# Weight splits on other engines, hidden copies on ScalarE, and a fourth raw tile in a fused attention and two-layer feed-forward kernel

## Chip, cores and metric

The kernel runs on one core of a Trainium2 chip. The metric is the device time of one execution in microseconds (us), lower is better. Five engines work side by side, each on its own queue in order: TensorE (PE, matmuls; PEld is its weight load), VectorE (DVE), ScalarE (ACT), GpSimd (POOL) and SyncE (SP), which here issues all DMAs.

## The reference, cut to what matters

```python
# q, k, v: (4, 8, 576, 64), f: (4, 8, 576), all float32; x: 2304 tokens x 512
scores = q @ k.T / 8 + (cum_i - cum_j)      # cum = cumsum(log(clip(f, 1e-4, 1)))
scores = where(causal, -1e9, scores)
attn = exp(scores - max) / (sum + 1e-9)
x = attn @ v                                # heads side by side: 2304 x 512
h = x @ w_in;  g = h * tanh(log1p(exp(h)));  x = g @ w_out      # layer 1, d_ff 2048
h = x @ w2_in; g = h * cos(h);               out = g @ w2_out   # layer 2
```

The four weight matrices arrive as 64-bit floats. The kernel makes two float32 values of each weight, a high part and the remainder, and likewise of each activation, and multiplies in three matmuls (high x high, high x low, low x high).

## The kernel before, in words

**Stages.** Attention works on jobs (a pair of heads of one batch) and on blocks of 128 queries. Beside it run "hidden units": one unit is 12 matmuls that make one 128-wide slice of layer 1's hidden values for 256, 288 or 320 tokens (L161). There are 128 of them; those that attention leaves over (31 or 32) run after it, from about 380 us on, and take all eight PSUM banks in turn. Each pair of units is copied from PSUM into a tile `hs`, the first half by ScalarE (L186), the second by VectorE (L188), and stored to `hd` in HBM by SP (L189). Then `ffn_units` goes through layer 1 in steps: it loads `hl` from `hd` (L223, seven steps ahead), applies the activation (L298), splits the result into gh (L324, ScalarE) and gl (L329, VectorE), and multiplies (L256). Layer 2 follows with L161, L301 to L329 and L264.

**Splitting the weights.** `split_weights` cuts each of the four matrices into 16 pieces of 512 KB. A piece is loaded into a `raw` tile (L109, on SP) and then goes through VectorE (L128, L129), GpSimd (L133, for the first matrix, called early) or ScalarE (L137, the others), VectorE (L138), ScalarE (L142, the high part wih or woh) and GpSimd (L143, the low part wil or wol, by subtraction). Only after L143 is the raw tile free for the next load. There are two raw tiles during attention and three after it; loads are issued one piece ahead during attention and two after it (`PF`). The early matrix is split during attention; then w1o (layer 1, out), w2i and w2o.

**Who calls it when.** During attention one piece is asked for every second block. In the loop over the left hidden units (L871) w1o's pieces are asked for in two of three units; from the fourth-last unit on, steps of `ffn_units` are interleaved. Then the loop over `ffn_units` asks for w2i and w2o.

**Order on the queues.** The program is written in this order, but a planner at build time arranges each engine's instructions by modelled durations; on the chip every engine then keeps that order. `issue_after(x)` puts an edge in that plan: the block's instructions on x's engine come behind x. `marks["v1"]` is the last VectorE instruction of a hidden unit or step, so the conversions' VectorE instructions stand behind it; the early ones stand behind the last softmax reduction (`marks["ttr"]`).

**Memory.** `ident`, `maskt` and `mask2` are used by attention alone but lie in the pool `const`, which stays for the whole kernel. Attention's own pool `att` is closed at L840, before the later raw pool is opened (L843).

```python
        PF = 1 if early else 2
                key = "ttr" if early else "v1"
                nc.gpsimd.tensor_tensor(out=lo[sl], in0=f(high), in1=f(hi[sl]), op=ALU.subtract)
    rawp = ctx.enter_context(tc.tile_pool(name="raw", bufs=3))
        if n % 3 != 2:
            next(w1o, None)
```

Of the kernel before, what the change touches and what calls it, by code (L numbers as in the profile page):

```python
# [9 lines left out]
F32 = mybir.dt.float32  # L10
F32R = mybir.dt.float32r
I32 = mybir.dt.int32
AF = mybir.ActivationFunctionType
ALU = mybir.AluOpType
# [21 lines left out]
def f(ap):  # L36
    return ap.bitcast(F32)
# [3 lines left out]
def tile_attention_two_ffn(  # L41
# [12 lines left out]
    nc = tc.nc  # L54
    B, H, S, D = q.shape
# [14 lines left out]
    const = ctx.enter_context(tc.tile_pool(name="const", bufs=1))  # L70
# [2 lines left out]
    raw_sb = ExitStack()  # L73
    rawp = raw_sb.enter_context(tc.tile_pool(name="raw0", bufs=2))

    ident = const.tile([128, 128], F32, name="ident")
    maskt = const.tile([128, S], F32, name="maskt")
    mask2 = const.tile([128, 320], F32, name="mask2")
    quarter = const.tile([128, 1], F32, name="quarter")

    hd = dram.tile([128, NJ, NT], F32, name="hd")
# [8 lines left out]
    marks, cums = {}, []  # L90

    def split_weights(layer, nm, pool, early=False):
        wi, wo = (w1_in, w1_out) if layer == 1 else (w2_in, w2_out)
        nb, nn = (NK, 256) if nm == "i" else (2, DM)
        per = 512 // nn
        pieces = []
        for c in range(NCH):
            if nm == "i":
                src = wi.bitcast(I32)[:, 512 * c : 512 * c + 512].rearrange("(b p) n -> p b n", p=128)
            else:  # L100
                src = wo.bitcast(I32)[256 * c : 256 * c + 256, :].rearrange("(b p) n -> p b n", p=128)
            pieces += [(c, src, u) for u in range(0, nb, per)]
        raws = {}

        def load(i):
            if i < len(pieces):
                c, src, u = pieces[i]
                raws[i] = rawp.tile([128, per, nn, 2], I32, tag="raw", name="raw")
                nc.sync.dma_start(out=raws[i].rearrange("p b n t -> p b (n t)"), in_=src[:, u : u + per])  # L109

        PF = 1 if early else 2
        with tc.issue_after(marks["cum"].ins):
            for i in range(PF):
                load(i)
        for i, (c, src, u) in enumerate(pieces):
            load(i + PF)
            raw = raws.pop(i)
            if u == 0:
                W[layer, c, nm] = tuple(
                    pool.tile([128, nb, nn], F32R, tag=f"w{nm}{x}{c}", name=f"w{nm}{x}{c}") for x in "hl"  # L120
                )
            hi, lo = W[layer, c, nm]
            with ExitStack() as hold:
                key = "ttr" if early else "v1"
                if key in marks:
                    hold.enter_context(tc.issue_after(marks[key].ins))
                high, low = raw[:, :, :, 1], raw[:, :, :, 0]
                nc.vector.tensor_scalar(out=low, in0=low, scalar1=29, scalar2=None, op0=ALU.logical_shift_right)  # L128
                nc.vector.scalar_tensor_tensor(  # L129
                    out=low, in0=high, scalar=-0x80000000, in1=low, op0=ALU.bitwise_and, op1=ALU.bitwise_or  # L130
                )
                if early:
                    nc.gpsimd.tensor_scalar(  # L133
                        out=f(high), in0=f(high), scalar1=REBIAS, scalar2=1.0, op0=ALU.mult, op1=ALU.mult
                    )
                else:
                    nc.scalar.activation(out=f(high), in_=f(high), func=AF.Copy, scale=REBIAS)  # L137
                nc.vector.scalar_tensor_tensor(  # L138
                    out=high, in0=high, scalar=3, in1=low, op0=ALU.logical_shift_left, op1=ALU.bitwise_or
                )  # L140
                sl = (slice(None), slice(u, u + per))
                nc.scalar.activation(out=hi[sl], in_=f(high), func=AF.Copy)  # L142
                nc.gpsimd.tensor_tensor(out=lo[sl], in0=f(high), in1=f(hi[sl]), op=ALU.subtract)  # L143
            if u + per == nb:
                converted[layer, c, nm] = clock["m"]
            yield

    def ripe(*key):
        return key in converted and clock["m"] - converted[key] >= WEIGHT_LAG
# [6 lines left out]
    def in_products(o, layer, j, xh, xl):  # L156
        wh, wl = weight(layer, j, "i")
        for kk in range(NK):
            wsl = (slice(None), kk, slice(128 * (j % 2), 128 * (j % 2) + 128))
            for i, (a, b) in enumerate(((wh, xh), (wh, xl), (wl, xh))):  # L160
                nc.tensor.matmul(  # L161
                    o, lhsT=a[wsl], rhs=b[:, kk, :],
                    start=(kk == 0 and i == 0), stop=(kk == NK - 1 and i == 2),
                )

    def hidden_units(tiles, p, hbank, ready):
        todo = {tl: 0 for tl in tiles}
        while todo:
            can = [tl for tl in todo if ready(sum(tl))]
            have = [tl for tl in can if ripe(1, todo[tl] // 2, "i")]  # L170
            if not can or not (have or attention_over):
                yield None
                continue
            t0, T = have[0] if have else min(can, key=todo.get)
            b, at = divmod(t0, S)
            xh, xl = (xb[b][:, x, :, at : at + T] for x in range(2))
            j0 = todo[t0, T]
            todo[t0, T] += 2
            if todo[t0, T] == NJ:
                del todo[t0, T]  # L180
            hs = p.tile([128, 2, 320], F32, tag="hs", name="hs")[:, :, 0:T]
            for j in (j0, j0 + 1):
                t = hbank()[:, 0:T]
                in_products(t, 1, j, xh, xl)
                if j == j0:
                    nc.scalar.activation(out=hs[:, 0], in_=t, func=AF.Copy)  # L186
                else:
                    marks["v1"] = nc.vector.tensor_copy(hs[:, 1], t)  # L188
                    nc.sync.dma_start(out=hd[:, j0 : j0 + 2, t0 : t0 + T], in_=hs)  # L189
                yield j  # L190

    def ffn_units(first, second, p, hlp, xp, hbank, abank, open_second):
# [552 lines left out]
            yield ("step", m, nxt[0] - m if nxt else 1)  # L745

    nc.scalar.preload_act_table_set("natural_log_exp_and_others")
    make_identity(nc, ident)
    nc.gpsimd.memset(quarter, 0.25)

    def make_masks():
        nc.gpsimd.memset(maskt, 0.0)
        nc.gpsimd.affine_select(
            out=maskt[:, S - 128 : S], in_=maskt[:, S - 128 : S], pattern=[[-1, 128]], base=0,
            channel_multiplier=1, compare_op=ALU.is_ge, fill=MASKED,
        )
        nc.gpsimd.memset(mask2, 0.0)
        for x in (0, 64):
            nc.gpsimd.affine_select(
                out=mask2[x : x + 64, 256:320], in_=mask2[x : x + 64, 256:320], pattern=[[-1, 64]], base=0,  # L760
                channel_multiplier=1, compare_op=ALU.is_ge, fill=MASKED,
            )
# [19 lines left out]
    def hbank():  # L782
        banks["n"] += 1
        n = banks["n"]
        if banks["wide"] and n % 2 == 0:
            return abank(n // 2 % NK)
        n = n // 2 if banks["wide"] else n
        if attention_over and n % 2:
            return psx.tile([128, 512], F32, tag="hx", name="hx", bufs=2)
        return psf.tile([128, 512], F32, tag="h", name="h", bufs=2)  # L790
# [8 lines left out]
        xps[i] = xsb[i].enter_context(tc.tile_pool(name=f"x{i}", bufs=1, side="right"))  # L799
    att_sb, att_ps, late_sb = ExitStack(), ExitStack(), ExitStack()  # L800
    ap = att_sb.enter_context(tc.tile_pool(name="att", bufs=2, side="right"))
    psf = ctx.enter_context(tc.tile_pool(name="ffps", bufs=1, space=PSUM))
    psa = att_ps.enter_context(tc.tile_pool(name="attps", bufs=6, space=PSUM))

# [3 lines left out]
    decay_tables(ap)  # L808
    att = attention_units(ap, bank)
    weights = split_weights(1, "i", w0p, early=True)  # L810
    done, done_tokens, attention_over = [], 0, False
    hid = hidden_units(hidden, hsp, hbank, lambda n: done_tokens >= n)
    credit = 0.0
    issued = 0
# [25 lines left out]
    att_sb.close()  # L840
    xsb[0].close()
    raw_sb.close()
    rawp = ctx.enter_context(tc.tile_pool(name="raw", bufs=3))  # L843
    attention_over = True
    psx = ctx.enter_context(tc.tile_pool(name="ffxps", bufs=1, space=PSUM))
    w1p = ctx.enter_context(tc.tile_pool(name="w1", bufs=1))
# [22 lines left out]
    banks["wide"] = True  # L869
    left = sum(NJ for _ in hidden) - issued  # L870
    for n, _ in enumerate(hid):  # L871
        if n % 3 != 2:
            next(w1o, None)
        if n == left - NK - 1:
            banks["wide"] = False
        if n >= left - 4:
            for kind, _ in ffn:
                if kind == "out":
                    break
# [38 lines left out]
```

## Time and profile before

| what | us |
|---|---|
| median of 3 runs | 1036.1 (1035.66 to 1036.38) |
| the profiled execution | 1035.64 |
| its span, first to last instruction | 1033.9 |
| TensorE busy | 1002.0 |
| VectorE busy | 595.3 |
| ScalarE busy | 526.4 |
| GpSimd busy | 232.6 |

The profile is of one execution. Busy time counts instructions that compute; issuing DMAs, branches and semaphores are not in it. "Granted clock" is the share of TensorE's full speed that the chip allowed. A number in brackets behind an instruction is the time that its engine sat idle before it, with what ended the wait. The chain of waits is followed back from the last instruction, at each step to what released it.

### The profile page before, as it was taken

How to read it: one execution, taken by the hardware profiler on the slowest of the kernel's cores; microseconds unless marked ns; L12 is line 12 of the kernel's file. 1: busy time of each engine (PE TensorE's matmuls, PEld its weight loads, DVE VectorE, ACT ScalarE, POOL GpSimd, SP SyncE). 2: the span in 40 equal slices, each digit the busy share in tenths (PEclk: the TensorE clock that was granted, in tenths of full speed). 3: DMA queues.
4: the chain of work that ended last, by engine and by line, in shares of the span. 5: the costliest groups of instructions: out<-in, count | busy, mean ns of one | idle time of the engine just before them, and what ended most of it. 6: DMA issues, size and time to landing. Idle time of an engine off the chain costs nothing.

```text
span 1033.9 us, 16608 instructions
## 1 busy us (share of the span) xinstructions
PE 1002.0 (97%) x5852; PEld 858.2 (83%) x5852; DVE 595.3 (58%) x1350; ACT 526.4 (51%) x1126; POOL 232.6 (22%) x303
## 2 busy tenths in 40 slices
PE   5997999999999999989999999999999999999998
PEld 4676789899999999878898888888888888888887
DVE  5875985555555437747773387665544444454454
ACT  4774765565555445456664466444333333333343
POOL 7655653323233104412220032111000000000000
PEclk9998999999999999999999999999999999999999
DMA  4663442323322158757885456202100200110010
GB/s 121 173 180 94 133 129 75 88 78 99 92 68 70 58 194 265 230 157 244 293 279 162 132 192 220 85 21 82 41 1 21 102 1 0 41 42 1 1 42 21
DMA packets 118494, 111.77 MB, mean 108 GB/s; under 512 B 66700, under 2 KB 87180, under 8 KB 118412
## 3 DMA queue, kind: packets, MB, share of 16 engines
q1 hardware_dynamic: 118412, 110.72, 35.0%
q8 instruction: 46, 0.75, 0.3%
q14 instruction: 36, 0.29, 0.1%
HBM read 77.49 MB, written 33.18 MB: 107 GB/s over the span
## 4 chain that ended last, share of the span: by engine, by line
PE 88%; POOL 4%; issue 3%; DVE 2%; DMA 2%; ACT 1%; SPq 0%; POOLq 0%; ACTq 0%; DVEq 0%
PE h L161 25%; PE acc L264 19%; PE acc L256 10%; PE hx L161 10%; PE s L637 5%; PE hx L256 4%; PE h L256 4%; PE s L527 4%; PE s L613 3%; PE s L470 2%; POOL wol L143 2%; PE s L521 2%; PE s L601 1%; DMA stk<-cumd 1%; DMA raw<-in_moe_w_out_dram 0%
## 5 line engine op out<-in xcount | busy, mean ns | idle before, releaser
L161 PE MATMUL h<-xb,wih 128*128 128x288 f32 (+2 forms) x848 | 183.0, 305 | 2.0 <-ACT wih L142 1.5
L161 PEld LDWEIGHTS h<-xb,wih 128*128 128x128 f32 x848 | 138.2, 190 | 8.2 <-issue 2.5
L161 PE MATMUL h<-xb,wil 128*128 128x288 f32 (+2 forms) x424 | 126.4, 301 | 4.9 <-POOL wil L143 4.9
L575 POOL TENSOR_SCALAR s<-s,sm 128x128 f32<-128x128 f32 (+4 forms) x144 | 83.7, 593 | 134.9 <-DVE sm L573 105.1
L264 PE MATMUL acc<-woh,gh 128*128 128x512 f32 x288 | 112.9, 392 | 0.0
L264 PE MATMUL acc<-woh,gl 128*128 128x512 f32 x288 | 112.3, 391 | 0.0
L264 PE MATMUL acc<-wol,gh 128*128 128x512 f32 x288 | 112.0, 389 | 0.0
L562 ACT ACTIVATE s<-s,mx 128x128 f32<-128x128 f32 (+4 forms) x144 | 83.6, 581 | 52.2 <-DVE mx L558 46.3
L558 DVE CUSTOM_DVE_ANT_0 s<-s,maskt 128x128 f32<-128x128 f32 (+4 forms) x144 | 66.9, 483 | 57.1 <-PE s L527 28.0
L329 DVE TENSOR_TENSOR gl<-hl,gh 128x512 fp32r<-128x512 f32 x72 | 58.5, 813 | 62.9 <-ACT gh L324 57.7
L161 PE MATMUL hx<-x,wih 128*128 128x512 f32 (+1 forms) x320 | 92.7, 369 | 0.0
L143 POOL TENSOR_TENSOR wol<-raw,woh 128x512 fp32r<-128x512 f32 x32 | 45.9, 1437 | 200.6 <-ACT woh L142 118.1
L315 ACT ACTIVATE n<-n 128x512 f32<-128x512 f32 (+1 forms) x80 | 47.1, 589 | 86.2 <-DVE n L309 86.1
L161 PE MATMUL h<-x,wih 128*128 128x512 f32 (+1 forms) x320 | 91.0, 369 | 0.0
L161 PEld LDWEIGHTS h<-xb,wil 128*128 128x128 f32 x424 | 80.4, 190 | 6.2 <-POOL wil L143 5.1
L329 DVE TENSOR_TENSOR gl<-e,gh 128x512 fp32r<-128x512 f32 (+1 forms) x80 | 54.0, 676 | 52.0 <-ACT gh L324 51.9
L308 DVE TENSOR_SCALAR n<-e 128x512 f32<-128x512 f32 (+1 forms) x80 | 32.7, 409 | 85.4 <-ACT e L301 84.9
L324 ACT ACTIVATE gh<-e 128x512 fp32r<-128x512 f32 (+1 forms) x80 | 47.0, 588 | 53.8 <-DVE e L320 49.2
L256 PE MATMUL acc<-gl,woh 128*128 128x512 f32 (+1 forms) x192 | 68.5, 358 | 0.7 <-DVE gl L329 0.7
L256 PE MATMUL acc<-gh,wol 128*128 128x512 f32 (+1 forms) x192 | 68.5, 358 | 0.0
L161 PEld LDWEIGHTS hx<-x,wih 128*128 128x128 f32 x320 | 58.4, 188 | 11.0
L161 PEld LDWEIGHTS h<-x,wih 128*128 128x128 f32 x320 | 58.4, 188 | 10.9
(119 smaller groups left out, 2164.3 us busy)
## 6 DMA issues: line engine op xcount, KB each, us to landing
hl<-hd SPq DMA_DIRECT2D x72, 256.0 KB
raw<-in_moe_w_in_dram SPq DMA_DIRECT2D x32, 512.0 KB
raw<-in_moe_w_out_dram SPq DMA_DIRECT2D x32, 512.0 KB
hd<-hs SPq DMA_DIRECT2D x48, 288.0 KB
yd<-stage SPq DMA_DIRECT2D x32, 256.0 KB
x<-yd SPq DMA_DIRECT2D x32, 256.0 KB
natk<-in_k_dram SPq DMA_DIRECT2D x32, 144.0 KB
out_dram<-stage SPq DMA_DIRECT2D x18, 256.0 KB
```

Source lines behind the costliest of these rows:

```text
L143: nc.gpsimd.tensor_tensor(out=lo[sl], in0=f(high), in1=f(hi[sl]), op=ALU.subtract)
L161: nc.tensor.matmul(o, lhsT=a[wsl], rhs=b[:, kk, :], start=(kk == 0 and i == 0), stop=(kk == NK - 1 and i == 2),)
L256: nc.tensor.matmul(acc[ti][d][:, 0:T], lhsT=a[dsl], rhs=b[:, gs], start=(start and i == 0), stop=(end and i == 2),)
L264: nc.tensor.matmul(acc[ti][m], lhsT=a[:, ms], rhs=b[:, j % 2, :], start=(start and i == 0), stop=(end and i == 2),)
L315: nc.scalar.activation(out=t, in_=t, func=AF.Sin, scale=TWO_PI)
L324: gmark[n] = nc.scalar.activation(out=gh, in_=e, func=AF.Copy)
L329: marks["v1"] = nc.vector.tensor_tensor(out=gl, in0=st.pop(n)[0], in1=f(gst[n][0]), op=ALU.subtract)
L527: marks["score"] = nc.tensor.matmul(o, lhsT=tails[x][j] if both else st[x][:, j, QS[i] : w], rhs=st[x + 1][:, j, c0:c1], start=(x == 0 and ...
L558: marks["ttr"] = nc.vector.tensor_tensor_reduce(out=s[:, c0:c1], in0=o, in1=mk, scale=-1.0, scalar=prev, op0=ALU.add, op1=ALU.min, accum_o ...
L562: nc.scalar.activation(out=s[:, 0:w], in_=s[:, 0:w], func=AF.Exp, scale=-1.0, bias=mx, accum_out=sm[:, j : j + 1])
L575: nc.gpsimd.tensor_scalar(out=s[:, 0:w], in0=s[:, 0:w], scalar1=sm[:, j : j + 1], scalar2=1.0, op0=ALU.mult, op1=ALU.mult)
L637: pair = nc.tensor.matmul(t[64 * j : 64 * j + 64, c0:width], lhsT=vt[jb][keys, c, j], rhs=pt[keys, j, c, c0:width], start=(c == 0), stop=( ...
```

## The change

- The subtraction L143 of the early pieces and of w1o's pieces goes from GpSimd to VectorE; w2i and w2o keep it on GpSimd.
- In the hidden units after attention both halves of `hs` are copied by ScalarE, and ScalarE issues the store to `hd`. During attention nothing changes there. w1o's pieces are held behind the last such copy (`marks["hs"]`, on ScalarE) in place of `marks["v1"]`.
- `ident`, `maskt` and `mask2` lie in attention's pool. The raw pool after attention has four tiles in place of three, and loads run three pieces ahead in place of two.
- In the loop over the left hidden units a piece of w1o is asked for in every second unit, in place of two of three.

```diff
-    ident = const.tile([128, 128], F32, name="ident")
-    maskt = const.tile([128, S], F32, name="maskt")
-    mask2 = const.tile([128, 320], F32, name="mask2")
...
-        PF = 1 if early else 2
+        PF = 1 if early else 3
...
-                key = "ttr" if early else "v1"
+                beside = (layer, nm) == (1, "o")
+                key = "ttr" if early else "hs" if beside else "v1"
...
-                nc.gpsimd.tensor_tensor(out=lo[sl], in0=f(high), in1=f(hi[sl]), op=ALU.subtract)
+                sub = nc.vector if early or beside else nc.gpsimd
+                sub.tensor_tensor(out=lo[sl], in0=f(high), in1=f(hi[sl]), op=ALU.subtract)
...
-                if j == j0:
-                    nc.scalar.activation(out=hs[:, 0], in_=t, func=AF.Copy)
+                if j == j0 or attention_over:
+                    marks["hs"] = nc.scalar.activation(out=hs[:, j - j0], in_=t, func=AF.Copy)
                 else:
                     marks["v1"] = nc.vector.tensor_copy(hs[:, 1], t)
-                    nc.sync.dma_start(out=hd[:, j0 : j0 + 2, t0 : t0 + T], in_=hs)
+                if j > j0:
+                    store = nc.scalar if attention_over else nc.sync
+                    store.dma_start(out=hd[:, j0 : j0 + 2, t0 : t0 + T], in_=hs)
...
+    ident, maskt, mask2 = (
+        ap.tile([128, w], F32, name=n, bufs=1) for n, w in (("ident", 128), ("maskt", S), ("mask2", 320))
+    )
+    make_identity(nc, ident)
+    nc.gpsimd.memset(quarter, 0.25)
...
-    rawp = ctx.enter_context(tc.tile_pool(name="raw", bufs=3))
+    rawp = ctx.enter_context(tc.tile_pool(name="raw", bufs=4))
...
-        if n % 3 != 2:
+        if n % 2 == 0:
             next(w1o, None)
```

## Rows read from the trace of the kernel before

**Rows 1.** The page: busy us, share, instructions; granted clock in 40 slices, in tenths

```profile
PE 1002.0 (97%) x5852; PEld 858.2 (83%) x5852; DVE 595.3 (58%) x1350; ACT 526.4 (51%) x1126; POOL 232.6 (22%) x303
...
PEclk9998999999999999999999999999999999999999
```

**Rows 2.** Stretches: us; busy PE, PEld, DVE, ACT, POOL; clock; DMA share, GB/s

```profile
25.00:150.00 125.00, 114.61 (x840) 91.62 (x839) 95.91 (x291) 83.81 (x229) 78.32 (x103) 0.97 0.53 141
87.00:94.00 7.00, 0.89 (x5) 0.69 (x5) 2.24 (x8) 2.43 (x6) 6.65 (x9) 0.88 0.13 28
94.00:100.00 6.00, 6.00 (x30) 5.89 (x32) 0.78 (x4) 0.38 (x1) 1.48 (x3) 0.57 0.40 131
...
380.00:443.00 63.00, 58.10 (x407) 55.63 (x406) 44.01 (x69) 33.56 (x61) 23.84 (x16) 1.00 0.80 249
448.00:1024.00 576.00, 576.00 (x2710) 482.10 (x2709) 313.77 (x505) 268.81 (x458) 43.09 (x32) 1.00 0.28 93
```

**Rows 3.** Who waited for whom, TensorE: us in total, times, longest

```profile
PE h L161 <- POOL wil L143: 4.9, 1, 4.9
...
PE hx L161 <- ACT hs L186: 2.5, 1, 2.5
...
PE acc L256 <- ACT gh L324: 2.1, 1, 2.1
...
PE acc L256 <- DVE gl L329: 0.7, 1, 0.7
```

**Rows 4.** GpSimd in order of time: start us, us, line, instruction [idle before]

```profile
91.91 0.50 POOL L507 CAST stkr<-stkr 64x384 fp32r<-64x384 f32 x1
92.50 1.29 POOL L143 TENSOR_TENSOR wil<-raw,wih 128x512 fp32r<-128x512 f32 x1
```

**Rows 5.** VectorE in order of time, around 90 us

```profile
95.96 0.42 DVE L188 COPY hs<-h 128x256 f32<-128x256 f32 x1 [5.91 <-PE h L161]
```

**Rows 6.** VectorE in order of time, a subtract without GpSimd beside it

```profile
448.20 0.69 DVE L329 TENSOR_TENSOR gl<-hl,gh 128x512 fp32r<-128x512 f32 x1 [3.54 <-ACT gh L324]
```

**Rows 7.** Chain of waits, matmuls of the hidden units: start us, us, what

```profile
93.84 5.28 PE h L161 x20
...
374.51 3.18 PE h L161 x24
```

**Rows 8.** One line's instructions, L129: duration ns min/median/max

```profile
L129 DVE SCALAR_TENSOR_TENSOR raw<-raw x64: 675/694/1853, 21.7 to 705.5; 128x512 int32<-128x512 int32 x64
```

**Rows 9.** Chain of waits, 370 to 450 us

```profile
431.27 1.33 POOL wol L143
...
432.62 4.89 DMA raw<-in_moe_w_out_dram
...
441.34 0.53 ACT gh L324
```

**Rows 10.** GpSimd in order of time, the last subtract of w1o

```profile
441.42 1.30 POOL L143 TENSOR_TENSOR wol<-raw,woh 128x512 fp32r<-128x512 f32 x1 [3.25 <-ACT woh L142]
```

**Rows 11.** Groups of VectorE, 380 to 443 us: busy us, mean ns, idle before

```profile
L129 DVE SCALAR_TENSOR_TENSOR raw<-raw 128x512 int32<-128x512 int32 x16 | 14.1, 880 | 0.4
```

**Rows 12.** TensorE in order of time, first L256 and last before its wait

```profile
431.48 0.40 PE L256 MATMUL acc<-gh,woh 128*128 128x512 f32 x1
...
439.46 0.39 PE L256 MATMUL acc<-gh,wol 128*128 128x512 f32 x1
```

**Rows 13.** Stretches of 2 us behind the wait

```profile
444.00:446.00 2.00, 2.00 (x7) 1.52 (x6) 0.67 (x1) 0.46 (x1) 0.00 (x0) 0.50 0.93 303
446.00:448.00 2.00, 2.00 (x8) 1.58 (x6) 0.00 (x0) 0.46 (x1) 0.00 (x0) 0.66 0.89 330
```

**Rows 14.** Groups of ScalarE, 380 to 443 us: hs copies

```profile
L186 ACT ACTIVATE hs<-hx 128x288 f32<-128x288 f32 x9 | 3.6, 397 | 0.6 <-ACT hs L186 0.6
```

**Rows 15.** L189, DMA issues on SP: duration ns min/median/max

```profile
L189 SPq DMA_DIRECT2D hd<-hs x64: 359/381/869, 55.4 to 439.6; - x64
```

**Rows 16.** Who waited for whom, all engines

```profile
DVE raw L138 <- ACT raw L137: 14.5, 28, 0.8
```

More of the change, by code (lines that the diff above doesn't have):

```diff
@@ L747, in tile_attention_two_ffn @@
     nc.scalar.preload_act_table_set("natural_log_exp_and_others")
-    make_identity(nc, ident)
-    nc.gpsimd.memset(quarter, 0.25)
     def make_masks():
```

## The prediction

> **What bounds the kernel now.** I read the busy times first. TensorE is busy for 1002.0 of 1033.9 us, and the granted clock is full in most of the 40 slices [rows 1]. Nearly all of the time is matmul work that the change does not touch; only the 31.9 us in which TensorE is idle, and the time at the lower clock, can go. The table by stretches says where these are: 10.4 us of idle time between 25 and 150 us, of which 6.1 from 87 to 94; a granted clock of 0.57 from 94 to 100; 4.9 us idle from 380 to 443; nothing at all from 448 to 1024 [rows 2]. The rest is the start and the tail, which the change leaves alone. The list of TensorE's waits puts names to the holes: once 4.9 us for the wil subtract on GpSimd (L143), and later 2.5 us for an hs copy on ScalarE, 2.1 for gh and 0.7 for gl [rows 3].
>
> **Place A, 87 to 100 us (the early subtracts go to VectorE).** GpSimd's order shows why wil is late: the subtract starts at 92.50, right behind a copy that ends at 92.41, and takes 1.29 [rows 4]; that copy follows the memsets of attention's second stack. VectorE is idle for the 5.91 us before 95.96, so from 90.05 on, because it waits for TensorE [rows 5]. There a subtract of the same shape (gl, L329) takes 0.69 us when nothing holds it up [rows 6]. So wil comes at about 90.8 where it came at 93.8: 3.0 us earlier. The 20 matmuls behind it took 5.28 us, to 99.12 [rows 7], at a clock of 0.57 over their stretch [rows 2]; at full clock they need 5.28 x 0.57 = 3.0. If the shorter pause keeps the clock, they end at 93.8, a gain of 5.3. The scores behind them need GpSimd's copy of 92.41, so 99.12 - 92.41 = 6.7 is the most that can come of it; if the clock still falls, 3.0 remains. I take 5.3.
>
> Against this stands VectorE's added work. All 16 early subtracts lie between 25 and 150 us: 16 x 0.69 = 11.0 us, or 16 x 0.865 = 13.8 at the mean of L129, the two-input VectorE instruction of the same size that runs beside GpSimd all through the kernel [rows 8]. VectorE is busy for 95.91 of these 125 us [rows 2], and of the 29.1 free ones some 9 lie in the hole itself and go with it. What VectorE loses is on the path only where TensorE already waits for it, and outside the hole TensorE's waits in this stretch are 10.4 - 6.1 = 4.3 us. I charge two subtracts, 1.4; the ends are 0 (all in free time) and 13.8 (all on the path). GpSimd gets back 16 x 1.29 us, but its normalises (L575) stand in no long wait of TensorE, so I credit nothing. Place A: 5.3 - 1.4 = 3.9.
>
> **Place B, 380 to 448 us (hidden units beside w1o's split).** The chain of waits at the seam reads: a GpSimd subtract ends at 432.60, only that frees a raw tile, its load takes 4.89, VectorE and ScalarE convert, and not before 441.34 can ScalarE turn to gh, which stands behind them on its queue [rows 9]. The subtract of the piece starts at 441.42 and takes 1.30 [rows 10], so one turn of a raw tile is 442.72 - 432.60 = 10.1 us, and three tiles give a piece per 3.4 us. The walk over the hidden units (24 matmuls, two units, in 3.18 us [rows 7]) asks for two pieces per three units, one per 2.4 us: the split never keeps up.
>
> After the change a turn has the same load and conversions and a VectorE subtract of 0.69 in place of 1.30: 9.5 us, by four tiles 2.4 us a piece. Besides, GpSimd has nothing left in this stretch, so L129, 0.880 on average here against a median of 0.694, loses 16 x 0.19 = 3.0 us [rows 8, 11]. The code asks for one piece per two units, 3.2 us; 16 pieces take 51 us from about 380, and TensorE ends the hidden units at 431.5 and has acc work until 439.9 [rows 12]. So a piece is ready before it is asked for, with about 8 us to spare before gh is due. The raw loads also stop queueing behind the hd stores on SP's queue. Freed are the waits of 2.5, 2.1 and 0.7 [rows 3] and the low clock behind the last: two stretches of 2 us at 0.50 and 0.66 lose 1.0 + 0.7 [rows 13]. That is 7.0 us.
>
> The cover is ScalarE. It is busy for 33.56 of the 63 us [rows 2] and gets 16 more hs copies at 0.40 [rows 14] and 16 stores. No row shows ScalarE issuing a DMA; SP needs 0.359 to 0.869 us, median 0.381, for each of these [rows 15], and a store could cost nothing if ScalarE only hands it on, so 0 to 13.9 us for all. I take SP's median, 6.1, for it is the same instruction. 33.6 + 6.4 + 6.1 = 46 of about 57 us: full, but not the bound. Every hs copy now stands in order behind L137 and L142, which wait for VectorE; the eight PSUM banks that the hidden units take in turn (12.7 us of TensorE work) cover that. I leave 1.0 for one such wait. Place B: 6.0, with 7.0 as the upper end and, if ScalarE falls behind, a loss as the lower.
>
> **The rest at nothing.** Identity and masks take 4 x (128 + 576 + 320) = 4096 bytes per partition, just one raw tile, so what is allocated behind stays where it was; the first instructions on GpSimd are the same. Three pieces ahead in the splits of w2i and w2o, and hs copies that no longer stand between VectorE's conversions, fall where TensorE is never idle [rows 2]. If the loads crowd out hl's, those still run seven steps ahead.
>
> **A rule against the change.** L129 takes 0.675 us at least and 1.853 at most [rows 8]. The Trainium skill, "SBUF — State Buffer", section "SBUF: two separate sides", says that a VectorE instruction with two SBUF inputs and a GpSimd one that reads SBUF lock each other out for a whole instruction. The trace agrees as far as L129's spread goes. By that rule an early subtract can stand still behind a normalise, while place B, without GpSimd, is free of it; the third rival prices this from the rows.
>
> **Sum.** The profiled execution took 1035.64 us (span 1033.9 and 1.7 around it), 0.46 below the median of 1036.1. 1035.64 - 3.9 - 6.0 = 1025.7, on the scale of the median 1026.
>
> **The rivals.**
> *Only B comes.* The subtracts cost attention what the hole gave back. For it: VectorE is busy for 77% from 25 to 150 us. Against: only 4.3 us of TensorE's waits there lie outside the hole. 1036.1 - 6.0 = 1030.
> *Only A comes.* ScalarE becomes the bound from 380 to 443, hs copies and gh come late, and TensorE waits at the seam as before. For it: 46 of 57 us on a queue in order. Against: the margin of 8 us. 1036.1 - 3.9 = 1032.
> *Slower: VectorE becomes the bound of attention.* Each early subtract waits in VectorE's order for ScalarE's wih (0.5 us, as L138 waited for ScalarE 14.5 us in 28 cases [rows 16]) and takes the 1.85 of L129's longest: 16 x 2.35 = 37.6 us. If half of the 29.1 free us is bound up in the dependences, TensorE starves for 37.6 - 14.5 = 23.1, less 5.3 and 6.0: 1048. It decides from (14.5 + 11.3) / 16 = 1.6 us for each subtract; the rows say 0.69 to 0.87.
> *It does not do what it says.* The order on each engine is drawn up at build time from modelled durations, and the new one can put a wait of the same size elsewhere. Against: the turn of a raw tile is arithmetic. 1035.5.
>
> **Chances.** Both places 0.51, only B 0.15, only A 0.12, no change 0.10, slower 0.12. The likeliest gives 1026 us, by itself 1022 (A 6.7 with no debit, B 7.0) to 1031. Eight times in ten I expect 1020 to 1036: both halves, part of the no-change case, and 2 us below for what a freer GpSimd may give and I could not price. A measurement of this kernel can tell 0.2%, 2.1 us. Faster 0.77, within it 0.11, slower 0.12.
>
> **What would show it.** Right: no GpSimd L143 before 443 us; no TensorE wait above 2 us around 90, and a full clock from there to the tail; w1o's pieces ending by about 432 and no wait for gh or gl when L256 starts. Wrong: TensorE waits of more than 5 us in sum for VectorE between 25 and 150 us, w1o's last L142 after the last hidden unit, or a wait of several microseconds where there was none.

## The result and the profile after

The changed kernel takes 1026.3 us in the median of 4 runs (1025.22 to 1028.19); the kernel before, run beside it, 1036.24 (1035.66 to 1036.81). The ratio is 0.9905 [0.989, 0.992]: faster by 9.8 us. The forecast was 1026.0. The profiled execution took 1025.59 us with a span of 1023.8.

The page of the kernel after, busy us, share and instructions, and the granted clock in 40 slices; it answers to [rows 1].

```profile
PE 998.6 (98%) x5852; PEld 854.2 (83%) x5852; DVE 593.8 (58%) x1367; ACT 529.8 (52%) x1141; POOL 195.4 (19%) x271
...
PEclk9999999999999999999999999999999999999999
```

TensorE's 5852 matmuls are the same, its busy time fell by 3.4 us, and the slice at the lower clock is gone. The other 6.7 us of the 10.1 that the span lost are idle time. The stretches of the kernel after (us; busy PE, PEld, DVE, ACT, POOL; clock; DMA share, GB/s), to be laid beside [rows 2], show where:

```profile
25.00:150.00 125.00, 117.10 (x874) 91.95 (x873) 103.84 (x314) 87.05 (x234) 65.32 (x91) 1.00 0.55 144
87.00:94.00 7.00, 6.37 (x49) 5.17 (x50) 4.07 (x14) 2.89 (x9) 5.24 (x8) 1.00 0.38 118
94.00:100.00 6.00, 5.07 (x43) 4.14 (x44) 4.47 (x14) 3.29 (x10) 2.51 (x5) 1.00 0.52 134
380.00:443.00 63.00, 62.38 (x417) 58.93 (x416) 38.92 (x64) 39.29 (x83) 0.00 (x0) 1.00 0.85 265
448.00:1014.00 566.00, 566.00 (x2666) 473.83 (x2665) 307.44 (x500) 264.35 (x450) 44.51 (x32) 1.00 0.28 93
```

From 87 to 94 us TensorE is busy for 6.37 us where it was busy for 0.89, and from 94 to 100 the clock is 1.00 where it was 0.57. From 380 to 443 it is busy for 62.38 instead of 58.10. GpSimd does nothing there any more, and ScalarE has 5.7 us more. From 448 us on neither kernel has idle time, up to 1014 us after and 1024 before.

TensorE's waits in the kernel after, 25 to 380 us (what waited, for whom: total us, times, longest), against [rows 3]:

```profile
PE s L638 <- DVE p L597: 2.2, 3, 0.8
PE h L160 <- ACT wih L140: 1.5, 1, 1.5
PE h L160 <- DVE wil L142: 1.2, 2, 0.7
PE h L160 <- DVE hs L187: 0.8, 1, 0.8
```

and from 380 to 450 us:

```profile
PE hx L160 <- ACT hs L185: 0.6, 1, 0.6
```

The 4.9 us for wil and the 2.1 and 0.7 us for gh and gl are gone, the 2.5 for hs is 0.6. In their place stand short waits for VectorE during attention; the 1.5 for wih were there before too.

### The profile page after: what moved, and what is told of

Read it like the earlier page. It is cut to its first block, busy times and chain, and to the rows that moved or that the text cites. A ratio compares the mean times of both kernels' runs of the same rounds, so it can differ in the third digit from the quotient of the medians.

```text
span 1023.8 us, 16547 instructions
## 1 busy us (share of the span) xinstructions
PE 998.6 (98%) x5852; PEld 854.2 (83%) x5852; DVE 593.8 (58%) x1367; ACT 529.8 (52%) x1141; POOL 195.4 (19%) x271
## 4 chain that ended last, share of the span: by engine, by line
PE 88%; DVE 4%; DMA 3%; POOL 2%; ACT 2%; issue 1%; ACTq 0%; SPq 0%; POOLq 0%
PE h L160 24%; PE acc L265 19%; PE acc L257 11%; PE hx L160 10%; PE s L638 4%; PE h L257 4%; PE hx L257 4%; PE s L528 4%; PE s L614 3%; PE s L471 2%; DMA raw<-in_moe_w_out_dram 2%; PE s L522 1%; PE s L602 1%; DVE raw L136 1%; DVE s L559 1%
## 5 line engine op out<-in xcount | busy, mean ns | idle before, releaser
L160 PE MATMUL h<-xb,wih 128*128 128x288 f32 (+2 forms) x848 | 180.9, 303 | 3.4 <-ACT wih L140 1.5
L576 POOL TENSOR_SCALAR s<-s,sm 128x128 f32<-128x128 f32 (+4 forms) x144 | 89.1, 632 | 153.2 <-DVE sm L574 121.8
L325 ACT ACTIVATE gh<-hl 128x512 fp32r<-128x512 f32 x72 | 45.3, 629 | 46.0 <-issue 28.5
```

The lines of the kernel that those rows point to most:

```text
L160: nc.tensor.matmul(o, lhsT=a[wsl], rhs=b[:, kk, :], start=(kk == 0 and i == 0), stop=(kk == NK - 1 and i == 2),)
L325: gmark[n] = nc.scalar.activation(out=gh, in_=e, func=AF.Copy)
L576: nc.gpsimd.tensor_scalar(out=s[:, 0:w], in0=s[:, 0:w], scalar1=sm[:, j : j + 1], scalar2=1.0, op0=ALU.mult, op1=ALU.mult)
```

## The experiments

The theory after the result was the prediction's own, with its two places kept apart: VectorE's early subtract closes the hole near 90 us, and at the seam the weight split of w1o now keeps pace. The rivals were that one part of the change does all of the work at the seam (a tile, a queue, or the lock between VectorE and GpSimd). Every kernel was timed beside the kernel before, whose medians were 1034.94, 1035.94 and 1035.01 us in the three groups of runs; ratios are to these.

### Place A alone, and all but place A

**e7_early_alone**: the kernel before, with

```diff
-                nc.gpsimd.tensor_tensor(out=lo[sl], in0=f(high), in1=f(hi[sl]), op=ALU.subtract)
+                sub = nc.vector if early else nc.gpsimd
+                sub.tensor_tensor(out=lo[sl], in0=f(high), in1=f(hi[sl]), op=ALU.subtract)
```

> The kernel before with only the early subtracts moved to VectorE. Queue theory: attention ends 3 to 4 us earlier (379.4 before), the seam near 440 us stays as it was with its 5 us of waits and low clock: about 1032.5 us. Rival (the added 11 us on VectorE cost what the hole gave back, and the gain of the whole change is the seam's): 1036 us. Re-plan theory: any value, attention's end not tied to the wait for wil.

Measured: 1032.11 us, 0.9969 [0.9958, 0.998], 3.2 us faster by the ratio.

**e1_early_on_gpsimd**: the kernel after, with

```diff
-                sub = nc.vector if early or beside else nc.gpsimd
+                sub = nc.vector if beside else nc.gpsimd
```

> The changed kernel with only the early subtracts put back on GpSimd. Queue theory (the hole at 87 to 100 us was the subtract standing behind the second stack's memsets): the wait of TensorE for wil near 90 us comes back with 4 to 5 us and the low clock behind it, attention ends 3 to 4 us later than in the changed kernel (376 us there), the rest is as there: about 1030 us. Re-plan theory (the new order of the instructions, not the engine of the subtract, closed the hole): no wait for wil, attention still ends near 376, 1026 us.

Measured: 1027.96 us, 0.9932 [0.9919, 0.9945], 7.0 us faster. TensorE's longest wait in it from 25 to 380 us is

```profile
PE h L160 <- POOL wil L142: 4.9, 1, 4.9
```

and the stretch behind the hole

```profile
94.00:100.00 6.00, 4.33 (x21) 4.33 (x22) 0.42 (x1) 0.38 (x1) 3.23 (x5) 0.59 0.43 131
```

The old wait and the low clock are back together. The two halves add up: 3.2 + 7.0 = 10.2 us against 9.8 for the whole. So place A is worth about 3 us and place B about 7. The profiles say the same: the last matmul of attention starts between 372.4 and 377.5 us in all nine kernels of this document that have the early subtract on VectorE (the kernel after 375.7, e7 376.0), and between 379.2 and 380.3 in all five that have it on GpSimd (before 379.2, e1 379.9).

### Which part works at the seam

**e3_three_tiles**: the kernel after, with

```diff
-        PF = 1 if early else 3
+        PF = 1 if early else 2
-    rawp = ctx.enter_context(tc.tile_pool(name="raw", bufs=4))
+    rawp = ctx.enter_context(tc.tile_pool(name="raw", bufs=3))
```

> The changed kernel with three raw tiles and loads two ahead, as before. Tile theory (the w1o split is bounded by the turn of a raw tile, about 9.4 us with the subtract on VectorE): 3.1 us a piece and not less, the last w1o conversion about 2 to 3 us later than in the changed kernel (434.3 us there), gh and gl as much later, the wait at the start of L256 comes back with 2 to 3 us and perhaps the low clock: 1028 to 1031 us. Pace theory (asking for a piece every second unit keeps the conversions out of gh's way, the fourth tile does nothing): 1026 us and no wait there.

Measured: 1029.96 us, 0.9952 [0.9939, 0.9965]. About half of the gain goes, though the runs scatter widely (1027.74 to 1031.99). TensorE's waits from 380 to 460 us in the profiled execution, the slowest of the six:

```profile
PE acc L257 <- ACT gh L325: 2.4, 1, 2.4
PE hx L160 <- ACT hs L185: 1.1, 1, 1.1
```

**e8_four_tiles_alone**: the kernel before, with masks and identity in attention's pool and

```diff
-        PF = 1 if early else 2
+        PF = 1 if early else 3
-    rawp = ctx.enter_context(tc.tile_pool(name="raw", bufs=3))
+    rawp = ctx.enter_context(tc.tile_pool(name="raw", bufs=4))
```

> The kernel before with only the memory part: identity and masks in attention's pool, four raw tiles, loads three ahead; subtracts on GpSimd, hs copies and stores and the pace as before. Tile theory: a turn of 10.1 us over four tiles is 2.5 us a piece, the last w1o subtract ends near 430 in place of 442.7, the waits of 2.5, 2.1 and 0.7 us and the low clock go: about 1030 us, attention's end unchanged. Pace theory: the conversions still end behind gh, 1035 to 1036 us.

Measured: 1035.1 us, 1.0004 [0.9995, 1.0013]. No gain at all: the tile theory failed in the time and in the hs wait, though the last subtract did start earlier, at 434.4 us in place of 441.4, and the waits for gh and gl went. The tile is needed, but alone it gives nothing. TensorE's only wait in e8 from 380 to 460 us is

```profile
PE hx L158 <- ACT hs L183: 5.2, 2, 4.7
```

and the stretch around it

```profile
425.00:450.00 25.00, 20.31 (x96) 17.88 (x95) 10.06 (x16) 9.87 (x18) 6.28 (x5) 0.86 0.66 205
```

It is a longer wait for an hs copy than before, with the clock at 0.86 behind it, where it was 0.93 in these 25 us before. The engines' own order in e8, in time (start us, us, instruction, idle time before it and what ended it), shows why. SP, which issues the raw loads behind the hd stores, and then VectorE and ScalarE:

```profile
422.05 0.38 SPq L186 DMA_DIRECT2D hd<-hs  x1
422.53 0.41 SPq L106 DMA_DIRECT2D raw<-in_moe_w_out_dram  x1
...
426.14 1.41 DVE L125 TENSOR_SCALAR raw<-raw 128x512 int32<-128x512 int32 x1 [0.96 <-DMA raw<-in_moe_w_out_dram]
427.47 0.68 DVE L135 SCALAR_TENSOR_TENSOR raw<-raw 128x512 int32<-128x512 int32 x1
...
428.18 0.67 ACT L139 ACTIVATE woh<-raw 128x512 fp32r<-128x512 f32 x1 [2.30 <-DVE raw L135]
428.83 0.67 ACT L134 ACTIVATE raw<-raw 128x512 f32<-128x512 f32 x1
430.80 0.69 ACT L139 ACTIVATE woh<-raw 128x512 fp32r<-128x512 f32 x1 [1.30 <-DVE raw L135]
431.40 0.39 ACT L183 ACTIVATE hs<-hx 128x288 f32<-128x288 f32 x1
```

A raw load goes out right behind a store, which itself waited for an hs copy on VectorE, so it arrives late; VectorE's conversion waits for it; ScalarE's conversions wait for VectorE; and the hs copy of 431.40, which TensorE needs, stands behind two of them. On a queue in order, a split that runs late delays the hidden units. That the store has to stand there is not shown by this: e12 below has the same wait with its stores on ScalarE.

**e2_w1o_on_gpsimd**: the kernel after, with

```diff
-                sub = nc.vector if early or beside else nc.gpsimd
+                sub = nc.vector if early else nc.gpsimd
```

> The changed kernel with w1o's subtract back on GpSimd (early subtracts stay on VectorE). Four tiles alone brought nothing, so two theories are left for the seam. Lock theory (VectorE's conversions are stretched by GpSimd's subtracts, 0.88 us for L129 where 0.69 is its median, and late conversions hold up hs copies and gh on ScalarE): L127 is stretched again, the split ends some 3 us later than in the changed kernel (434.3 us), waits for hs or gh of 2 to 4 us return: 1028 to 1031 us. Queue theory (raw loads stood on SP's queue behind hd stores, which waited for VectorE's hs copies): stores stay on ScalarE, so nothing returns: 1026 us.

Measured: 1024.29 us, 0.9895 [0.9877, 0.9914]: no loss against the whole change, and no wait of TensorE from 380 to 460 us. The stretch that the lock theory foretold came (L127 takes 1.113 us in the mean), but not its waits.

**e5_hs_as_before**: the kernel after, with

```diff
-                key = "ttr" if early else "hs" if beside else "v1"
+                key = "ttr" if early else "v1"
-                if j == j0 or attention_over:
+                if j == j0:
-                    store = nc.scalar if attention_over else nc.sync
+                    store = nc.sync
```

> The changed kernel with the hidden units' hs copies, stores and the conversions' hold as before (second half on VectorE, store on SP, hold behind VectorE's last copy); four tiles and subtracts on VectorE stay. Queue theory: raw loads wait behind stores again, TensorE waits for hs of 3 to 5 us, 1029 to 1032 us. Lock theory: without GpSimd beside it VectorE has room for 16 copies of 0.45 us more, so at most 1 us is lost: 1026 to 1027 us.

Measured: 1025.18 us, 0.9901 [0.9883, 0.9918].

**e6_store_on_sp**: of e5's edits the last one alone.

> The changed kernel with only the hd stores after attention put back on SP; both hs copies stay on ScalarE. Queue theory: raw loads behind stores that wait for ScalarE, a part of the waits returns: 1028 to 1030 us. Lock theory: nothing changes, ScalarE saves 16 issues of 0.37 us: 1026 us or up to 1 us less.

Measured: 1025.39 us, 0.9902 [0.9879, 0.9925]. Neither e5 nor e6 costs anything, though in both the raw loads queue behind the stores again. So neither SP's queue nor the VectorE copies explain e8 by themselves.

**e4_pace_as_before**: the kernel after, with

```diff
-        if n % 2 == 0:
+        if n % 3 != 2:
```

> The changed kernel with w1o's pieces asked for in two of three units, as before. If the pace matters (pieces asked for faster than they come block hs copies and gh on ScalarE's queue): waits for hs of 1 to 3 us, 1027 to 1029 us. If only the speed of the pieces matters: the last piece's place in the order is no later, gh comes no later, 1025 to 1026 us.

Measured: 1024.67 us, 0.9897 [0.9879, 0.9915]. The slower pace is not needed either, so long as the rest of the change is there.

### Two intervals that race

Three of the four parts at the seam could each be left out at no cost, and the fourth was useless by itself. That asked for another account. A piece is *asked for* every 2.39 us (two of three units, 24 matmuls or two units in 3.18 us [rows 7]) or, in the new pace, every 3.18. It is *delivered* in whatever time loads, conversions and the subtract take. If delivery is slower than asking, the lag grows over 15 intervals and should end in hs or gh waits; if not, there should be none. Three further kernels test this.

**e11_pace_alone**: the kernel before with the new pace (`n % 2 == 0`) and nothing else.

> The kernel before with the pace of one piece every second unit and nothing else. Race theory: 3.42 us delivered against 3.18 asked, late by 15 x 0.24 = 3.6 us at the last piece, so a part of the waits stays: 1 to 3 us of waits for hs or gh, 1031 to 1034 us. Pace theory (the order of asking does it all): no wait, 1028 to 1029 us. Relief theory: 1035 us.

Measured: 1032.36 us, 0.9972 [0.9963, 0.9982]; as expected.

**e10_four_tiles_and_pace**: e8 with the new pace.

> The kernel before with the memory part (identity and masks in attention's pool, four raw tiles, three ahead) and the pace of one piece every second unit; subtracts on GpSimd, hs copies and stores as before. No single undoing of subtract, hs or pace brought the seam's waits back, so a new theory: the race of two intervals. The walk asks for a piece every 2.39 us (two of three units) or 3.18 us (every second); the chip delivers one in 3.42 us before, 2.93 with four tiles, 3.0 in the changed kernel. Where it delivers more slowly than it is asked, hs copies and gh get stuck behind late conversions; where it keeps up, nothing waits, whatever engine does the work. Race: 2.93 against 3.18, no wait for hs or gh after 380 us, 1035 - 5 of waits - 2 of clock: 1027 to 1030 us. Rival (relief of VectorE or of SP's queue is needed): 1034 to 1035 us, as four tiles alone.

Measured: 1031.32 us, 0.9964 [0.995, 0.9978], 1.3 us above the upper end of the expected range. The hs wait is gone, as the race theory had it; gh (1.0 us) and gl (0.7) are late again, which it had not. The profiled execution (1033.3 us) is 2.0 us above the median.

**e12_gpsimd_and_old_pace**: the kernel after, with e2's and e4's edits together. Each of them alone cost nothing.

> The changed kernel with w1o's subtract on GpSimd and the pace of two in three units; each of these alone cost nothing. Race theory: delivered every 2.9 us against 2.39 asked, late by 15 x 0.5 = 7.6 us, waits for hs or gh of 2 to 5 us return: 1027 to 1031 us. Rival (four tiles and hs copies on ScalarE suffice): no wait, 1024 to 1025 us.

Measured: 1033.01 us, 0.9981 [0.9972, 0.999]. Of the 9.8 us some 2 are left (1035.01 - 1033.01), less than expected. The wait came back as the race theory had it, and it is e8's again, in e12's waits from 380 to 460 us:

```profile
PE hx L160 <- ACT hs L185: 5.1, 2, 4.5
```

The table takes the first and last start of w1o's subtract in the profile of each kernel; delivered is their distance over 15, lag 15 x (delivered - asked). "Seam" is the time from the start of attention's last matmul to the end of the span, so it leaves place A out.

| kernel | asked, us | delivered, us | lag, us | TensorE's waits, 380 to 460 us | seam, us | ratio |
|---|---|---|---|---|---|---|
| before | 2.39 | 3.42 | 15.4 | hs 2.5, gh 2.1, gl 0.7 | 654.7 | 1 |
| e7, VectorE early alone | 2.39 | 3.51 | 16.8 | hs 3.0, gh 1.2, gl 0.7 | 654.2 | 0.9969 (with A) |
| e8, tiles alone | 2.39 | 2.93 | 8.1 | hs 5.2 | 655.3 | 1.0004 |
| e12 | 2.39 | 2.78 | 5.9 | hs 5.1 | 654.9 | 0.9981 (with A) |
| e4, old pace | 2.39 | 2.60 | 3.2 | hs 0.2 | 647.6 | 0.9897 (with A) |
| e11, pace alone | 3.18 | 3.41 | 3.5 | hs 1.7, gh 0.6, gl 0.6 | 651.0 | 0.9972 |
| e3, three tiles | 3.18 | 3.27 | 1.4 | hs 1.1, gh 2.4 | 652.7 | 0.9952 (with A) |
| e10, tiles and pace | 3.18 | 3.18 | 0 | gh 1.0, gl 0.7 | 651.2 | 0.9964 |
| after | 3.18 | 3.05 | below 0 | hs 0.6 | 648.1 | 0.9905 (with A) |
| e6, store on SP | 3.18 | 3.05 | below 0 | none | 648.3 | 0.9902 (with A) |
| e1, all but A | 3.18 | 2.99 | below 0 | none | 647.1 | 0.9932 |
| e2, GpSimd subtract | 3.18 | 2.90 | below 0 | none | 647.1 | 0.9895 (with A) |
| e13, below | 3.18 | 2.89 | below 0 | none | 647.1 | 0.987 (with A) |
| e5, hs as before | 3.18 | 2.84 | below 0 | none | 647.1 | 0.9901 (with A) |

Every kernel with a lag above 5 us waits 2.5 us or more for hs, and its seam is as long as before; every one without a lag waits 0.6 or less for hs. Four tiles bring delivery from 3.4 to 2.9 us, which is still slower than the old pace asked for, and so e8 waits. With four tiles, the new pace takes the lag to 0 (e10), and VectorE's subtract at the old pace takes it to 3.2 us (e4). The wait does not grow with the lag (15.4 us of lag wait 2.5, 5.9 wait 5.1), and between 1 and 4 us the lag alone does not decide (e4 waits 0.2 in all, e3 3.5): how a lag falls out as hs or gh waits depends on where in ScalarE's order the hs copies stand, and for that no run here gives a rule. A delivered interval below the asked one is no faster split; it reads as a late first piece that was caught up.

A second condition, found after these runs, rules gh: the last piece must be converted on ScalarE before TensorE has used up its prepared acc steps, 8.2 us behind the first. It is missed in the kernel before, e7, e11, e3 and e10, and in these five alone does TensorE wait for gh. So the two conditions part the fourteen kernels into a seam of 654 to 655 us (lag above 5 us), 651 to 653 (a smaller lag or none, but gh late) and 647 to 648 (neither). This fits every profile, but the lag is read from the same profiles as the waits, and of the three kernels foretold from it only e11 came out within its range of times. The planner draws up a new order for each kernel, and no run holds the order fixed; that the order did it in one or the other is not excluded.

e12 loses the whole of place B: its seam is 654.9 us, the kernel before's 654.7, the kernel after's 648.1. The hs waits explain 5.1 of these 6.8 us; for the rest the clock of 0.86 in the 25 us from 425 leaves room. The 2 us that e12 keeps are place A's. So two edits that each cost nothing alone cost all 7 us of the seam together.

### A version faster than both

**e13_later_use**: e2 with the first use of an early piece put off by two more steps.

```diff
-WEIGHT_LAG = 4
+WEIGHT_LAG = 6
-                sub = nc.vector if early or beside else nc.gpsimd
+                sub = nc.vector if early else nc.gpsimd
```

> The changed kernel with w1o's subtract on GpSimd (the fastest so far, 1024.3 us) and early weights used two half-blocks later (6 in place of 4 after their conversion in the order of asking). In attention TensorE still waits 1.5 us for wih near 87 us, after which the clock falls in a part of the executions. If that wait is the weight being used too soon after its conversion: it goes, no fall of the clock there, 1022 to 1023.5 us. If the order gets worse because fewer units are at hand early: 1025 us or more.

Measured: 1021.33 us, 0.987 [0.9855, 0.9885], 3.0 us below e2 (2.6 by the ratios) and the fastest of all. Its mechanism was not the expected one. TensorE's longest waits in e13 from 25 to 380 us:

```profile
PE h L160 <- ACT wih L140: 1.5, 1, 1.5
PE s L638 <- DVE p L597: 1.4, 2, 0.8
```

Its stretches, with the columns as above:

```profile
25.00:150.00 125.00, 120.12 (x891) 96.16 (x890) 102.49 (x316) 87.26 (x235) 63.85 (x91) 0.99 0.56 147
87.00:94.00 7.00, 6.93 (x44) 6.31 (x44) 3.26 (x12) 2.42 (x8) 4.76 (x7) 0.76 0.38 115
```

The wait for wih near 87 us stays, and the clock is down to 0.76 behind it. What went are the waits for wil and for hs on VectorE (1.2 and 0.8 us in the kernel after) and one of the three for p: TensorE's idle time from 25 to 150 us is 125 - 120.12 = 4.9 us, against 8.5 in e2. In size this is the debit of place A, taken back. No run gives the later use to the kernel before, so how much of it would come there too, with the subtracts on GpSimd, is not shown.

## Why the prediction was right, step by step

**Place A, the hole: right in kind, more gained and more given back.** Forecast: 5.3 gained, 1.4 lost, 3.9 in sum. VectorE took wil's subtract at 87.50 us, not at 90.05, because the planner put it between the copies into attention's stack. Of the kernel after, VectorE, and of the kernel before, TensorE, in time:

```profile
87.50 0.68 DVE L142 TENSOR_TENSOR wil<-raw,wih 128x512 fp32r<-128x512 f32 x1
...
98.92 0.69 PE L527 MATMUL s<-stkr 128*128 128x128 f32 x4
```

The scores behind the hole start at 91.61 instead of 98.92, 7.3 us earlier; the hole itself began 0.8 earlier, so 6.5 belong to it, near the upper bound of 6.7. That bound was the right one: these scores no longer wait for weights but for GpSimd. The chain of waits of the kernel after (start us, us, what):

```profile
86.89 1.11 POOL stkr L674
...
88.05 1.05 POOL stkr L679
...
89.16 1.06 POOL stkr L680
...
90.28 1.28 POOL stkr L508 x2
91.56 0.04 issue
91.61 0.68 PE s L528 x4
```

At the last matmul of attention 3.5 of the 7.3 us are left (374.13 us against 377.62). The 3.8 given back are the debit, which I had at 1.4. It lies where the prediction put it, in TensorE's waits in this stretch: its idle time from 25 to 150 us outside 87 to 94 rose from 4.3 to 125 - 117.10 - 0.63 = 7.3 us, 3.0 more. VectorE's busy time rose by 7.9 us there. The charge of two subtracts was too small: the rows showed how much VectorE was free, but not how soon its results would be used. Waits for wil itself are 1.2 us of it, an hs copy on VectorE 0.8, and 2.2 are waits for copies of p, of which at least one stands right behind an early subtract on VectorE's queue (VectorE, then TensorE, kernel after):

```profile
96.12 0.69 DVE L142 TENSOR_TENSOR wil<-raw,wih 128x512 fp32r<-128x512 f32 x1
96.73 0.55 DVE L597 COPY p<-s 128x384 f32<-128x384 f32 x1
...
97.33 0.88 PE L638 MATMUL s<-p,natv 128*64 128x128 f32 x12 [0.78 <-DVE p L597]
```

These are more than the 3.0, because waits of the kernel before for stkr, xb and cumd fell away or shrank. In e13 a later first use, with the subtracts where they are, takes as much idle time away as the debit put in.

**Place B, the seam: 6.0 forecast, 7.0 by e1.** The waits of 2.1 and 0.7 and the low clock are gone, of the 2.5 for hs 0.6 remains. In the profiles, from the last matmul of attention to the end, the time fell by 656.3 - 649.7 = 6.6 us (counted here from the start of the last 20 matmuls).

**The working of place B was less sound than its sum.** Two steps failed.

The margin of "about 8 us to spare before gh is due" was under 1 us. ScalarE, VectorE and TensorE at the seam of the kernel after, each in time:

```profile
432.87 0.67 ACT L140 ACTIVATE woh<-raw 128x512 fp32r<-128x512 f32 x1 [0.21 <-DVE raw L136]
433.45 0.62 ACT L325 ACTIVATE gh<-hl 128x512 fp32r<-128x512 f32 x1
...
434.19 0.68 DVE L330 TENSOR_TENSOR gl<-hl,gh 128x512 fp32r<-128x512 f32 x1
...
426.13 0.40 PE L257 MATMUL acc<-gh,woh 128*128 128x512 f32 x1
...
434.34 0.63 PE L257 MATMUL acc<-gh,woh 128*128 128x512 f32 x2
```

gh is done at 433.45 + 0.62 = 434.07, and TensorE turns to it at 434.34. I had held the new split against the old due time. The gain itself moves the due time: the first acc matmul came at 426.13 and not at 431.48, 5.4 us earlier, and so did the end of the prepared work. The rest of the margin went in the pieces' later end: the last subtract ends at 434.3, not near 431. It cost nothing here, but e10 and e3 show the other side of the edge. One sign that the prediction had set for being wrong did come: w1o's last high part (L142 before, L140 here) starts at 432.87, behind the last hidden unit, whose matmuls end about when the first acc matmul starts, at 426.13. It did no harm, because the prepared acc steps cover 8.2 us.

And the argument set against the case of no change, that "the turn of a raw tile is arithmetic", was wrong: four tiles alone gave nothing in e8. Nor does the turn stay as long as it was when a tile is added: 10.1 us over four tiles would be 2.5 us a piece, and e8 delivers one per 2.93; with VectorE's subtract the forecast was 2.4, and e4, which asks that fast, gets 2.60. What counts is the turn against the pace asked for, and which queue the late piece stands on. The relief of SP's queue, which the prediction also named, was worth nothing that e6 could show. With the pace slowed to 3.18 us the sum came out, but that part of the change was priced at nothing by itself; e11 gives it 2.9 us by itself (ratio 0.9972, 1.9 to 3.8 us by its interval).

**The cover held.** ScalarE's stores take as long to issue as SP's. One line's instructions in the kernel after, 380 to 443 us (min/median/max ns):

```profile
L190 ACTq DMA_DIRECT2D hd<-hs x15: 366/366/380, 386.7 to 432.0; - x15
```

ScalarE in time, where such a store falls:

```profile
397.23 0.71 ACT L140 ACTIVATE woh<-raw 128x512 fp32r<-128x512 f32 x1 [1.57 <-DVE raw L136]
397.24 0.37 ACTq L190 DMA_DIRECT2D hd<-hs  x1
```

and a group of VectorE in the same stretch (busy us, mean ns, idle before):

```profile
L127 DVE SCALAR_TENSOR_TENSOR raw<-raw 128x512 int32<-128x512 int32 x12 | 8.3, 689 | 0.2
```

The forecast had 0.381 us for a store from [rows 15], and charged all 16 to ScalarE. But 8 of these 15 issues run, as the one shown, while a ScalarE instruction computes, so the charge of 6.1 us was too high; ScalarE computes for 39.29 of the 63 us. With GpSimd idle L127 fell to 0.689 us, as the prediction had it from [rows 8, 11].

**The rivals.** "Only B" and "only A" were priced at 1030 and 1032; e1 and e7, which have these two outcomes made by hand, gave 1028 and 1032. The slower rival needed 1.6 us for each early subtract; TensorE's waits for VectorE from 25 to 380 us are 2.2 + 1.2 + 0.8 + 0.4 = 4.6 us in all, just below the 5 that were set as the mark.

## What to carry to other kernels

A gain upstream moves the due time of what is behind it: compare a transfer's new end with the new due time, not with the old one. Where several small edits each shorten a feeder, lay the interval at which it delivers beside the interval at which it is asked; while it delivers more slowly than it is asked, every late piece can block whatever stands behind it on an in-order queue, and some more speed may be worth nothing (e8); once it keeps up, undoing edits one at a time shows no loss until the line is crossed again (e2, e4 and then e12). To see whether an engine has room for more work, look at how soon its result is used and not only at its free time.

## What the hardware showed that was not expected

**GpSimd's subtract costs VectorE nearly as much as doing it.** VectorE's three conversions of w1o in e2, from 385 to 430 us (instructions, busy us, mean ns):

```profile
L136 DVE SCALAR_TENSOR_TENSOR raw<-raw 128x512 int32<-128x512 int32 x16 | 14.9, 932 | 8.0 <-ACT raw L135 8.0
L127 DVE SCALAR_TENSOR_TENSOR raw<-raw 128x512 int32<-128x512 int32 x12 | 13.4, 1113 | 0.4
L126 DVE TENSOR_SCALAR raw<-raw 128x512 int32<-128x512 int32 x12 | 5.2, 430 | 4.5 <-DMA raw<-in_moe_w_out_dram 4.3
```

With GpSimd idle the same 40 instructions take 16 x 0.689 + 12 x 0.689 + 12 x 0.428 = 24.4 us; here 33.5. The 9.1 us more are close to the 16 x 0.689 = 11.0 us that the subtracts take on VectorE itself. In e12 it is partly L126, with one input, that is held up: its durations (min/median/max ns, 385 to 430 us) are

```profile
L126 DVE TENSOR_SCALAR raw<-raw x12: 417/771/1540, 395.6 to 425.4; 128x512 int32<-128x512 int32 x12
```

One of the long ones, of 1.52 us, runs from 425.36 us on beside a GpSimd subtract of 425.17 to 426.59. The Trainium skill, "SBUF — State Buffer", section "SBUF: two separate sides", has an exclusive lock, held for a whole instruction, between GpSimd and a VectorE instruction with two SBUF inputs or in a two-port mode. The stretches of L127 and L136, with two inputs, agree with it; whether L126 runs in such a mode no run here shows. Little of the time given to GpSimd was taken off VectorE there.

**The clock behind a pause of 1.5 us near 87 us differs between executions.** In the profiled executions of e3, e4, e5 and e13 the granted clock over 87 to 94 us is 0.76; in those of the kernel after, e2, e6, e7 and e12, which wait 1.5 us for wih at the same place, it is 1.00. In e5 the two stretches behind the pause (88 to 90, 90 to 92 us) show

```profile
88.00:90.00 2.00, 2.00 (x11) 2.00 (x11) 0.98 (x2) 0.51 (x2) 1.88 (x3) 0.52 0.61 138
90.00:92.00 2.00, 2.00 (x11) 2.00 (x10) 0.00 (x0) 0.00 (x0) 1.91 (x4) 0.63 0.74 264
```

near the lower of the two levels, 1.2 of 2.4 GHz. They lose 2 x 0.48 + 2 x 0.37 = 1.7 us, about the distance between the two pairs of runs of the kernel after (1025.2 and 1025.6 us at a mean clock of 1.000, 1027.0 and 1028.2 at 0.998). That these are the same thing was not shown: only one of the four was profiled, and in e6 a run at 1.000 took 1026.7 us and one at 0.997 took 1024.95.
